# Loads, weight joins and look-ahead products moved in the first three steps of a linear-attention and feed-forward kernel

## Chip, cores and metric

The kernel runs on one core of one Trainium2 chip. The metric is the device time of one execution in microseconds (us). Matrix products run on TensorE (PE in the profile; its weight loads are PEld), elementwise work on VectorE (DVE), ScalarE (ACT) and GpSimd (POOL). SyncE (SP) only issues DMAs. Each engine works through its own queue in the order in which the program was written, because the kernel is built under a manual schedule. Semaphores are put in by the framework wherever one instruction needs what another makes, or its buffer.

## What is computed

```python
# r, k, v, w: (4, 8, 768, 48); u: (8, 48)
for t in range(S):
    cur = np.einsum('bhd,bhe->bhde', u[None] * kt, vt)
    y[:, :, t] = np.einsum('bhd,bhde->bhe', rt, state + cur)
    state = wt[:, :, :, None] * state + np.einsum('bhd,bhe->bhde', kt, vt)
x = y.transpose(0, 2, 1, 3).reshape(B * S, H * D)     # (3072, 384)
h = x @ w_in                                          # w_in (384, 2048), float64 as given
sp = np.maximum(h, 0.0) + np.log1p(np.exp(-np.abs(h)))
out = (h * erf(sp)) @ w_out                           # w_out (2048, 384), float64 as given
```

## The kernel before

The sequence is cut into six chunks of 128 tokens and the four batches into two pairs. This makes twelve steps; step `s` handles chunk `s // 2` of batch pair `s % 2`.

**Attention.** `attend_first` handles step 0, `attend` steps 1 to 4, and `attend_late` the rest. Inside a step the recurrence over time is done by halving: there are six levels. At each level PE makes 64 small products (`level_products`, L537), DVE multiplies the later halves of r and k by decay totals, in place (`scale`, L327), and DVE or ACT merges the products into the matrix `own` (`take_level`, L549 and L556). The products of level n need the scaling of level n-1, and the scaling of level n overwrites what the products of level n read. POOL makes the decay totals ahead (L349 in the first two steps, L401 in `prepare`). After level six come `from_own` (own times v into the PSUM tile `y`, L571), transposes (L896), `state_part` (L643) and `through_state` (L597), which gives xT, the transposed input of the feed-forward part. Six small DMAs fill a last part of xT (L629).

**Feed-forward.** Its work is cut into pieces that stand between the levels on PE. `hidden` of step s-1 makes the first product, 12 matmul instructions to a piece (L985). `project` of step s-3 makes the second, 8 matmul instructions to a piece (L1017). `place(n)` is called at the end of each level and issues the pieces: one hidden piece in steps 1 and 2; in step 3 two projection pieces after each of the levels one to four. From step 3 on, `project` of step 0 reads `w_out_sb`: the last two of its eight pieces, issued after level four, read its row blocks 12 to 15. The last step's projection is `project_fast`, seven products of half width with sums made by DVE (L1113, L1117).

**Weights.** They come as float64 words and are converted in 16 pairs of row blocks, 0 to 7 for `w_in_sb` and 8 to 15 for `w_out_sb`. A pair passes five stages: `l` loads the words (two DMAs, L147), `b` scales the high words on ACT into `y` (L247, L249), `r` scales the low words on ACT into a buffer `rest` (L255), `h` shifts on DVE (L264, and for pairs from 8 on a second instruction, L269), and `o` adds the rest on POOL (L277). `j` (join) is `h` and `o`. The table `CONVERT` says for each step and level which stages are sent, each time for the next pair of that stage. The first string of an entry goes out ahead of `take_level` (`early`), the second inside `place`.

**Rows for step 4.** From step 4 on, the first levels are made from rows instead. `load_rows` loads them, and `prepare(s + 1)`, a generator that is resumed once in each level of step s from level two on, multiplies them on DVE. In step 3 it is resumed between `take_level` and `place`; its resumption in level three runs from L469 on.

```python
            if level > 1 and (s, level) != (DIRECT, LOG - 1):
                next(following, None)
            place(level - 1)
```

**Buffers.** The tiles `in`, `w` and `v` have two buffers each, `words` three, `rest` two. SP issues loads in program order, so an issue that waits for a buffer holds back those behind it. `load_second`, `load_step`, `load_v` and `load_w` issue the loads of the steps.

Of the kernel before, what the change touches and what calls it, by code (L numbers as in the profile page):

```python
# [17 lines left out]
P = 128  # L18
FAST = 3
EP = 64  # L20
HC = 64
# [40 lines left out]
def kernel(  # L62
# [111 lines left out]
        nc.scalar.copy(t[:, 0, 0, 0:1], behind)  # L174
        load_halves(t, rkw[1])

    def load_v(s, behind=None):

        vt = loaded[s][1]
        if behind is not None:  # L180
            nc.gpsimd.tensor_copy(out=vt[:, 0, 0:1], in_=behind)
        nc.sync.dma_start(out=vt[:], in_=v[s])

    def load_step(s):
        t = ins.tile([P, 2, JP, C], FP32, name="in")
        vt = ins.tile([P, NH, D], FP32, name="v")
        if s < DIRECT:
            load_halves(t, rkw[s])
        else:
            nc.sync.dma_start(out=t[:], in_=rkw[s][:, 0:2])  # L190
        if s <= DIRECT:
            load_w(s)
        if s == 2:
            nc.sync.dma_start(out=block_sb[:], in_=block_mask)
            nc.sync.dma_start(out=u_row[:], in_=u_rows)
        loaded[s] = t, vt
        if s > 2:
            load_v(s)
# [16 lines left out]
    def convert(weights):  # L215

        held = {}
        plain = weights[0][1].dtype == FP32  # L220
        signed = len(weights) // 2

        def load(i, behind=None):
            if i >= len(weights):
                return
            dst, src = weights[i]
            if plain:
                nc.sync.dma_start(out=dst, in_=src)
                return
            words = wide.tile([P, 2, DM, 2], I32, name="words", bufs=3)  # L230
            if behind is not None:
                nc.gpsimd.tensor_copy(out=words[:, 0, 0, 0:1].bitcast(FP32), in_=behind)
            load_halves(words[:].rearrange("p i n two -> p i (n two)"), src.bitcast(I32))
            held[i] = {"words": words}

        def scale_high(i, part=slice(0, 2)):


            if i not in held:
                return  # L240
            if i < 2:
                base = ps_m.tile([P, NP * C], FP32, name="m")[:, :DM]
            else:
                base = y[:].rearrange("p e j q t -> p e (j q t)")[:, :, :DM]
            high = held[i]["words"][:, part, :, 1].bitcast(FP32)
            if i < signed:
                nc.scalar.activation(base, high, AF.Prelu, scale=2.0**-112, alpha=-(2.0**32))  # L247
            else:
                nc.scalar.mul(out=base, in_=high, mul=2.0**-112)  # L249
            held[i].setdefault("bases", []).append((base.bitcast(I32), part))  # L250

        def scale_low(i):
            if i in held:
                rest = wide.tile([P, 2, DM], I32, name="rest", bufs=2)
                nc.scalar.mul(  # L255
                    out=rest[:], in_=held[i]["words"][:, :, :, 0].bitcast(U32), mul=2.0**-29
                )
                held[i]["rest"] = rest

        def shift(i):  # L260
            if i in held:
                base, part = held[i]["bases"].pop(0)
                into = weights[i][0].bitcast(I32)[:, part]
                nc.vector.tensor_scalar(  # L264
                    out=into if i < signed else base, in0=base, scalar1=3, scalar2=None,
                    op0=ALU.logical_shift_left,
                )
                if i >= signed:
                    nc.vector.scalar_tensor_tensor(  # L269
                        out=into, in0=held[i]["words"][:, part, :, 1], scalar=-(1 << 31),  # L270
                        in1=base, op0=ALU.bitwise_and, op1=ALU.bitwise_or,
                    )

        def add(i):
            if i in held:
                into = weights[i][0].bitcast(I32)
                nc.gpsimd.tensor_tensor(  # L277
                    out=into, in0=into, in1=held.pop(i)["rest"][:], op=ALU.add
                )

        def join(i):
            shift(i)
            add(i)

        stages = {"l": load, "b": scale_high, "r": scale_low, "h": shift, "o": add, "j": join}
        done = {"l": 4, "b": 2, "r": 2, "j": 2}

        def send(what):
            for stage in what:
                stages[stage](done[stage])  # L290
                done[stage] += 1

        return stages, send
# [436 lines left out]
    def attend_first(xT):  # L730
# [20 lines left out]
        def wait_for(t):  # L751

            nc.gpsimd.tensor_copy(out=block_sb[:, 0:1], in_=in_t[:, 0, JP - 1, t : t + 1])
# [8 lines left out]
        for level in range(2, LOG):  # L762
            pp = turns.pop("pp", None) or products([P, NE, JP, HC])
            level_products(pp, RK, level)
            scale(0, level)
            turns["pp"] = products([P, NE, JP, HC])
            keep_busy(turns["pp"])
            take_level(own, pp, level)
            if level == 2:
                stages["b"](0, 0)  # L770
                stages["b"](0, 1)
                stages["r"](0)
                for _ in prepare(1):
                    pass
                stages["l"](1, own[:, 0, 2:3])
                nc.sync.dma_start(out=vt[:], in_=v[0])
                nc.sync.dma_start(out=ws[1][:], in_=rkw[1][:, 2])
            elif level < LOG - 1:
                stages["h"](0)
            if level in behind:  # L780
                wait_for(1 << level - 1)
                totals(*behind[level])
        totals = plan_totals(1)
        pp = turns.pop("pp")
        level_products(pp, RK, LOG)
# [27 lines left out]
        nc.scalar.copy(middle[rows(1)], ps[0][1][rows(1), :, :D])  # L813
        nc.vector.tensor_copy(middle[rows(0)], ps[0][0][rows(0), :, :D])
        stages["r"](1)
        stages["h"](1)
        stages["h"](1)
        wait_for(HC - 1)
        stages["o"](0)
        nc.gpsimd.tensor_mul(faded[1][:], middle[:], ends[:, :, 1:2].to_broadcast([P, JP, D]))  # L820
        load_v(1, middle[:, 0, 0:1])
        totals(1)
        stages["o"](1)
        totals(*range(2, LOG + 1))
# [28 lines left out]
    def attend(s, xT, early, place, behind):  # L853
# [10 lines left out]
            next(following)  # L864
        for level in range(near_log(s) + 1 if s == DIRECT else 1, LOG + 1):
            rk = made[:] if level == 1 else RK
            pp = products([P, NE, JP, HC])
            if s == level == 1:
                level_products(pp, rk, level, range(NP))
                turns.pop("hop")()  # L870
                level_products(pp, rk, level, range(NP, JP))
                send("br")
            else:
                level_products(pp, rk, level)
            if level == LOG and s == DIRECT:
                spread_blocks(s + 1, pp)
            scale(s, level)
            if s == 1 and level == 2:
                turns.pop("pending")()
                load_v(2)  # L880
            early(level - 1)
            got = pp[:].rearrange("p e n t -> p (e n) t")
            if level == 1:
                nc.vector.tensor_mul(
                    own[:], got, first[:, None, :].to_broadcast([P, NH, HC])
                )
            else:
                take_level(own, pp, level)
            if level > 1 and (s, level) != (DIRECT, LOG - 1):
                next(following, None)  # L890
            place(level - 1)

        from_own(s, own, 1)
# [184 lines left out]
    def project_fast(s, gs):  # L1078
# [34 lines left out]
        nc.vector.tensor_add(halves, halves, m0[:, None, lo].to_broadcast([P, 2, ND]))  # L1113
        nc.sync.dma_start(out=out[i * NJ + 1, c], in_=o[1][:])
        yield
        product(m1[:, lo], a12, b21, True)
        nc.vector.tensor_add(o[0][:], o[0][:], m1[:])  # L1117
        nc.sync.dma_start(out=out[i * NJ, c], in_=o[0][:])
        yield

    xTs, hids, projs = {}, {}, {}
# [58 lines left out]
    def run_late(s, tokens, following=None):  # L1180
# [26 lines left out]

    CONVERT = (
        (),
        (("j", "brl"),) * 5 + (("j", "l"), ("", ""), ("", ""), ("", "brl")),  # L1210
        (("", "jbrl"),) * 5 + (("", "j"), ("", ""), ("", ""), ("", "br")),
        (("", "jbr"), ("", "j")),
    )

    STAGES = {
# [17 lines left out]
    with tc.manual_schedule(  # L1233
# [15 lines left out]
        for s in range(n_steps):  # L1249
# [3 lines left out]
            def convert_at(n, late=True):  # L1253
                if s < len(CONVERT) and n < len(CONVERT[s]):
                    send(CONVERT[s][n][late])

            def place(n):
# [7 lines left out]
                if s in ALONE:  # L1265
                    if s == 2 and not n:

                        next(hids[0])
                    convert_at(n)
                    advance(STAGES[s][n])  # L1270
                else:
                    advance(STAGES[s][n])
                    convert_at(n)
                beside(s, next(places))

            def run(n, following):
# [12 lines left out]
                )  # L1289
            else:  # L1290
                attend_first(xTs[s])
            if s + 2 < n_steps:
                load_step(s + 2)
                if s + 2 == DIRECT:
                    load_rows(s + 2)
        s = n_steps
        from_own(s - 1, ready[s - 1][0], 1)
        fence()
# [102 lines left out]
```

## Time and profile before

| what | value |
|---|---|
| median of 3 runs (lowest, highest) | 598.27 us (597.46, 601.87) |
| the profiled execution, its own time | 599.54 us |
| its span, first to last instruction | 597.7 us |
| mean granted TensorE clock | 0.997 |
| busy share of the span: PE, PEld, DVE, ACT, POOL | 98%, 84%, 73%, 60%, 45% |
| DMA, mean over the span | 106 GB/s |

The span and what lies around it (1.8 us) make the profiled execution's time, and that stood 1.27 us above the median. Matmuls are pipelined and their ends are modelled, so PE's 98% doesn't mean that it ran at its peak; a gap between its weight loads shows a stall better. In the timeline each line gives the start and the duration in us, engine and source line, operation, output and inputs, count, and in brackets the idle time before it with what ended that. "issue" there means that the engine waited for nothing that the profile shows.

### The profile page before, as it was taken

How to read it: one execution, taken by the hardware profiler on the slowest of the kernel's cores; microseconds unless marked ns; L12 is line 12 of the kernel's file. 1: busy time of each engine (PE TensorE's matmuls, PEld its weight loads, DVE VectorE, ACT ScalarE, POOL GpSimd, SP SyncE). 2: the span in 40 equal slices, each digit the busy share in tenths (PEclk: the TensorE clock that was granted, in tenths of full speed). 3: DMA queues.
4: the chain of work that ended last, by engine and by line, in shares of the span. 5: the costliest groups of instructions: out<-in, count | busy, mean ns of one | idle time of the engine just before them, and what ended most of it. 6: DMA issues, size and time to landing. Idle time of an engine off the chain costs nothing.

```text
span 597.7 us, 16615 instructions
## 1 busy us (share of the span) xinstructions
PE 583.5 (98%) x7264; PEld 500.3 (84%) x7264; DVE 436.6 (73%) x518; ACT 361.6 (60%) x473; POOL 270.9 (45%) x306
## 2 busy tenths in 40 slices
PE   8889999999999999999999999999999999999997
PEld 6667787678758857898898898898898898898997
DVE  6757498799996799799799799799799525023140
ACT  3546777817534398675765765766666664746710
POOL 3447265510579549749549549449449100000000
PEclk9989999999999999999999999999999999999999
DMA  7685382531304324335334334334331300000000
GB/s 238 229 305 174 103 287 74 218 129 32 136 31 148 77 99 168 72 107 168 71 108 168 71 107 168 72 106 133 72 107 53 72 9 26 2 21 13 2 27 27
DMA packets 53937, 63.24 MB, mean 106 GB/s; under 512 B 35144, under 2 KB 40424, under 8 KB 52840
## 3 DMA queue, kind: packets, MB, share of 16 engines
q1 hardware_dynamic: 53480, 61.98, 32.6%
q8 instruction: 57, 0.93, 0.7%
q10 hardware_dynamic: 384, 0.20, 0.1%
q14 instruction: 16, 0.13, 0.1%
HBM read 52.39 MB, written 8.69 MB: 102 GB/s over the span
## 4 chain that ended last, share of the span: by engine, by line
PE 80%; DVE 13%; DMA 3%; issue 2%; ACT 1%; POOL 0%; SPq 0%; DVEq 0%; POOLq 0%; ACTq 0%
PE m L985 36%; PE m L1093 28%; PE m L1017 5%; PE pp L537 4%; DVE in L327 3%; PE y L571 2%; PE pp L643 2%; PE y L597 1%; DVE h L974 1%; DVE own L549 1%; DVE words L466 1%; DVE sums L452 1%; DVE y L264 1%; DVE rk L462 1%; DMA rest<-in_w_rows 1%
## 5 line engine op out<-in xcount | busy, mean ns | idle before, releaser
L985 PE MATMUL m<-xT,w_in_sb 128*128 128x256 f32 x1152 | 258.7, 383 | 1.0 <-DMA xT<-y 0.9
L985 PEld LDWEIGHTS m<-xT,w_in_sb 128*128 128x128 f32 x1152 | 216.9, 191 | 32.7 <-issue 1.3
L994 ACT COPY h<-m 128x512 f32<-128x512 f32 x96 | 55.7, 581 | 83.2 <-PE m L985 83.2
L327 DVE TENSOR_TENSOR in<-in,tot_sb 128x1024 f32<-128x1024 f32 (+1 forms) x59 | 78.3, 1327 | 26.1 <-PE pp L537 16.1
L462 POOL TENSOR_TENSOR rk<-words 128x528 f32<-128x528 f32 (+3 forms) x28 | 41.6, 1486 | 91.6 <-DVE sums L452 81.2
L466 POOL TENSOR_TENSOR words<-words,rest 128x528 f32<-128x528 f32 (+10 forms) x77 | 79.1, 1027 | 6.0
L1017 PE MATMUL m<-w_out_sb,h 128*128 128x384 f32 x192 | 64.3, 491 | 0.0
L1017 PEld LDWEIGHTS m<-w_out_sb,h 128*128 128x128 f32 x192 | 35.7, 190 | 23.6
L1093 PE MATMUL m<-mixed,h 128*128 128x192 f32 x288 | 51.1, 331 | 0.0
L1093 PE MATMUL m<-w_out_sb,h 128*128 128x192 f32 x288 | 50.3, 329 | 0.0
L941 ACT ACT_TABLE_LOAD x36 | 46.2, 1283 | 2.6 <-issue 2.0
L1093 PEld LDWEIGHTS m<-w_out_sb,h 128*128 128x128 f32 x288 | 46.9, 190 | 0.5
L1093 PEld LDWEIGHTS m<-mixed,h 128*128 128x128 f32 x288 | 46.6, 190 | 0.9
L945 ACT ACT_TABLE_LOAD x36 | 46.2, 1283 | 1.6 <-DVE room L1076 1.1
L537 PEld LDWEIGHTS pp<-in 48*64 48x64 f32 (+1 forms) x2368 | 33.6, 126 | 12.8 <-issue 6.8
L1093 PE MATMUL m<-w_out_sb,room 128*128 128x192 f32 x256 | 44.2, 326 | 0.0
L1093 PEld LDWEIGHTS m<-w_out_sb,room 128*128 128x128 f32 x256 | 42.0, 190 | 0.0
L950 DVE TENSOR_TENSOR h<-h,y 128x1024 f32<-128x1024 f32 x17 | 20.7, 1215 | 28.3 <-ACT y L945 28.2
L537 PE MATMUL pp<-in 48*64 48x64 f32 (+1 forms) x2368 | 37.9, 213 | 2.0 <-DVE in L327 2.0
L941 ACT ACTIVATE room<-h 128x1024 f32<-128x1024 f32 x36 | 38.1, 1057 | 0.4
L950 DVE TENSOR_TENSOR h<-h,pp 128x1024 f32<-128x1024 f32 x19 | 23.0, 1213 | 19.5 <-ACT pp L945 19.5
L462 POOL TENSOR_TENSOR words<-words 128x336 f32<-128x336 f32 (+6 forms) x49 | 35.2, 719 | 3.8
(141 smaller groups left out, 820.2 us busy)
## 6 DMA issues: line engine op xcount, KB each, us to landing
in<-in_rkw SPq DMA_DIRECT2D x8, 1024.0 KB, 6.0
words<-in_moe_w_in SPq DMA_DIRECT2D x16, 384.0 KB, 5.6
words<-in_moe_w_out SPq DMA_DIRECT2D x16, 384.0 KB, 4.7
words<-in_rk_rows SPq DMA_DIRECT2D x8, 768.0 KB, 5.6
w<-in_rkw SPq DMA_DIRECT2D x11, 512.0 KB, 7.4
v<-in_v SPq DMA_DIRECT2D x12, 384.0 KB, 5.8
out<-o SPq DMA_DIRECT2D x24, 192.0 KB, 2.8
in<-in_rkw SPq DMA_DIRECT2D x7, 512.0 KB, 5.9
```

The lines of the kernel that those rows point to most:

```text
L327: nc.vector.tensor_mul(halves, halves, view(tots[level - 1], 0, [[1, n], [2, nb], [0, half]]))
L462: engine.tensor_mul(terms[n], r[:, :, n:], k[:, :, : near - n])
L466: engine.tensor_mul(k[:, :, :m], k[:, :, :m], w[:, :, n : n + m])
L537: nc.tensor.matmul(pp[s0 : s0 + m, e, n, :m], lhsT=rk[rows(e), 1, n, s0 : s0 + m], rhs=rk[rows(e), 0, n, t0 : t0 + m], start=True, stop=True,)
L571: nc.tensor.matmul(y[at(e, p), e, j, p // 2, t], lhsT=vt[t, n * NE + e, :], rhs=own[t, e * JP + n, :], start=swap == 1 and not j and not q ...
L941: nc.scalar.activation(sp_room, chunks[0], AF.Softplus)
L945: nc.scalar.activation(at, sp_room, AF.Erf)
L950: nc.vector.tensor_mul(h, h, at)
L985: nc.tensor.matmul(ps[:, ff, :], lhsT=w_in_sb[:, g * FG + f + ff, kk * P : (kk + 1) * P], rhs=xT[:, kk, :], start=kk == 0, stop=kk == KT - 1,)
L994: nc.scalar.copy(h[:, f : f + FT, :], ps[:])
L1017: nc.tensor.matmul(ps[j][:], lhsT=gs[g][:, f, j * C : (j + 1) * C], rhs=w_out_sb[:, g * FG + f, :], start=g + f == 0, stop=g == NG - 1 and ...
L1093: nc.tensor.matmul(to, lhsT=a[:, f], rhs=b[:, f], start=start and f == 0, stop=f == FG - 1, skip_group_check=True,)
```

## The change

- `load_w(2)` and `load_v(1)` are issued in step 0 after level two. The POOL copy that held `load_v(1)` back goes.
- The rest of `load_step(2)` moves from the end of step 0 to step 1, level two, after the pending state product. The two small loads of `block_sb` and `u_row` move from step 2's load to step 3's. `load_rows(4)` moves from the end of step 2 to step 3, level one, after that level's join.
- The words of pair 4 are loaded in step 0, after stage `r` of pair 1, instead of in step 1.
- In `attend_first` the wait and the totals of a level come ahead of the other work of the level.
- In step 1, level six, the join of pair 7 comes ahead of `scale`.
- In step 2 the products of level two are issued right after the last piece of `hidden(0)`, ahead of that level's piece of `hidden(1)`.
- `CONVERT`: step 1 no longer loads in level one. In step 2, stages `b` and `r` of pair 13 leave level five for the end of the step, and its join leaves level six for level one of step 3. So pairs 13, 14 and 15 are joined in levels one, two and three of step 3, where pairs 14 and 15 were joined in levels one and two.
- The last sum of the last step is made and stored in two halves, the upper one ahead of the last product.

```diff
-    def load_v(s, behind=None):
+    def load_v(s):
 
         vt = loaded[s][1]
-        if behind is not None:
-            nc.gpsimd.tensor_copy(out=vt[:, 0, 0:1], in_=behind)
         nc.sync.dma_start(out=vt[:], in_=v[s])
...
-        if s <= DIRECT:
+        if 2 < s <= DIRECT:
             load_w(s)
-        if s == 2:
+        if s == 3:
             nc.sync.dma_start(out=block_sb[:], in_=block_mask)
             nc.sync.dma_start(out=u_row[:], in_=u_rows)
...
-        done = {"l": 4, "b": 2, "r": 2, "j": 2}
+        done = {"l": 5, "b": 2, "r": 2, "j": 2}
...
             take_level(own, pp, level)
+            if level in behind:
+                wait_for(1 << level - 1)
+                totals(*behind[level])
             if level == 2:
...
                 nc.sync.dma_start(out=ws[1][:], in_=rkw[1][:, 2])
+                load_w(2)
+                load_v(1)
             elif level < LOG - 1:
                 stages["h"](0)
-            if level in behind:
-                wait_for(1 << level - 1)
-                totals(*behind[level])
...
         stages["r"](1)
+        stages["l"](4)
         stages["h"](1)
...
-        load_v(1, middle[:, 0, 0:1])
         totals(1)
...
-            pp = products([P, NE, JP, HC])
+            pp = turns.pop("pp", None) or products([P, NE, JP, HC])
...
-            else:
+            elif s != 2 or level != 2:
                 level_products(pp, rk, level)
             if level == LOG and s == DIRECT:
                 spread_blocks(s + 1, pp)
+            if s == 1 and level == LOG:
+                early(level - 1)
             scale(s, level)
             if s == 1 and level == 2:
                 turns.pop("pending")()
+                load_step(2)
                 load_v(2)
-            early(level - 1)
+            if s != 1 or level < LOG:
+                early(level - 1)
...
+            if s == 2 and level == 1:
+
+                def ahead():
+                    turns["pp"] = products([P, NE, JP, HC])
+                    level_products(turns["pp"], RK, 2)
+
+                turns["ahead"] = ahead
             place(level - 1)
...
-        product(m1[:, lo], a12, b21, True)
-        nc.vector.tensor_add(o[0][:], o[0][:], m1[:])
-        nc.sync.dma_start(out=out[i * NJ, c], in_=o[0][:])
+        parts = (hi, lo) if s == n_steps - 1 else (slice(0, DM),)
+        for part in parts:
+            if part is parts[-1]:
+                product(m1[:, lo], a12, b21, True)
+            nc.vector.tensor_add(o[0][:, part], o[0][:, part], m1[:, part])
+            nc.sync.dma_start(out=out[i * NJ, c, :, part], in_=o[0][:, part])
...
-        (("j", "brl"),) * 5 + (("j", "l"), ("", ""), ("", ""), ("", "brl")),
-        (("", "jbrl"),) * 5 + (("", "j"), ("", ""), ("", ""), ("", "br")),
-        (("", "jbr"), ("", "j")),
+        (("j", "br"),) + (("j", "brl"),) * 4 + (("j", "l"), ("", ""), ("", ""), ("", "brl")),
+        (("", "jbrl"),) * 4 + (("", "jl"), ("", ""), ("", ""), ("", ""), ("", "br")),
+        (("", "jbr"), ("", "jbr"), ("", "j")),
...
                         next(hids[0])
+                        turns.pop("ahead")()
                     convert_at(n)
...
                     convert_at(n)
+                    if s == DIRECT - 1 and not n:
+                        load_rows(DIRECT)
...
-            if s + 2 < n_steps:
+            if s and s + 2 < n_steps:
                 load_step(s + 2)
-                if s + 2 == DIRECT:
-                    load_rows(s + 2)
```

## The prediction

> **What bounds the kernel now.** I read the page first, then the windows, then the timeline of steps 0 to 3 and of the end.
>
> ```profile
> PE 583.5 (98%) x7264; PEld 500.3 (84%) x7264; DVE 436.6 (73%) x518; ACT 361.6 (60%) x473; POOL 270.9 (45%) x306
> PE 80%; DVE 13%; DMA 3%; issue 2%; ACT 1%; POOL 0%; SPq 0%; DVEq 0%; POOLq 0%; ACTq 0%
> ```
>
> PE carries 80% of the chain that ended last. Work taken off another engine gains only where PE stands still; a new wait on PE costs its full length. So I list PE's stalls in the first 130 us. The windows (columns PE, PEld, DVE, ACT, POOL busy, then the granted clock) show two places:
>
> ```profile
> 36.05:39.47 3.42, 1.57 (x13) 1.38 (x14) 1.30 (x4) 0.00 (x0) 0.00 (x0) 1.00 0.68 245
> 39.47:42.89 3.42, 3.42 (x24) 2.33 (x26) 2.31 (x2) 2.05 (x3) 1.82 (x1) 0.50 0.97 329
> 109.60:126.00 16.40, 16.40 (x171) 10.08 (x172) 16.13 (x16) 9.15 (x8) 8.90 (x9) 1.00 0.35 144
> ```
>
> PE stood for half of one window and then had half its clock for the next 3.42 us. From 109.6 to 126, in step 3, DVE is busy 16.13 of 16.40 us: it has no room there. The timeline names the stalls of steps 0 to 2:
>
> ```profile
> 14.71 1.23 DVE L327 TENSOR_TENSOR in<-in,tot_sb 128x1024 f32<-128x1024 f32 x1 [0.96 <-POOL tot_sb L349]
> ...
> 30.34 0.54 PEld L537 LDWEIGHTS pp<-rk 48*64 48x64 f32 x26 [1.24 <-issue]
> ...
> 37.90 0.25 PEld L643 LDWEIGHTS pp<-v,kT 64*48 64x48 f32 x7 [2.56 <-issue]
> 38.21 4.29 PE L985 MATMUL m<-xT,w_in_sb 128*128 128x256 f32 x12
> 43.71 2.86 PE L985 MATMUL m<-xT,w_in_sb 128*128 128x256 f32 x12
> ...
> 58.40 0.55 PEld L571 LDWEIGHTS y<-own,v 64*48 64x48 f32 x32 [1.00 <-issue]
> ...
> 69.42 0.30 PEld L985 LDWEIGHTS m<-xT,w_in_sb 128*128 128x128 f32 x2 [1.28 <-issue]
> ...
> 92.64 0.66 PEld L571 LDWEIGHTS y<-own,v 64*48 64x48 f32 x32 [1.17 <-ACT own L556]
> ```
>
> And step 3, where weights meet the projection:
>
> ```profile
> 117.52 2.68 POOL L277 TENSOR_TENSOR w_out_sb<-w_out_sb,rest 128x768 int32<-128x768 int32 x1
> 119.05 1.96 DVE L469 TENSOR_TENSOR words<-words,u_row 128x768 f32<-128x768 f32 x1
> 122.42 5.43 PE L1017 MATMUL m<-w_out_sb,h 128*128 128x384 f32 x16
> 125.43 0.56 DVE L466 TENSOR_TENSOR words<-words,rest 128x384 f32<-128x384 f32 x1
> 125.91 1.22 DVE L327 TENSOR_TENSOR in<-in,tot_sb 128x1024 f32<-128x1024 f32 x1
> ```
>
> Pair 15 is finished on POOL at 120.20. Only then come the row products of step 4 on DVE, 119.05 to 125.99, and the last two projection pieces on PE at 122.42, which read it.
>
> **What the Trainium skill says.** "Runtime: NRT & Kernel Launch", Instruction fetch mechanics: instructions come in blocks of 256, the next one fetched by DMA while the current one runs, "mostly hidden". Here it is not hidden twice: from the break before 30.34 to that before 37.90 PE issues 127 weight loads, 127 matmuls and 2 waits, one block, and no operand was missing. The 57 instruction packets of queue 8 on the page fit 14,528 such instructions. "TensorE: Matmul & The Clock Gate", What's actually happening: after an idle window of about 3.4 us the clock is halved until a busy window has passed; the two windows above agree. "PSUM — Partial Sum Buffer", PSUM bank collisions: a bank is to be guarded as a whole, whatever columns are touched; no line of before shows DVE and PE at different columns of one bank. "SBUF — State Buffer", SBUF: two separate sides: DVE with two SBUF inputs and POOL exclude each other for a whole instruction; L277 takes 1.83 us alone and 2.68 at 117.52, beside L327.
>
> **The change, part by part**, against the profiled execution.
>
> *Totals ahead (step 0).* POOL's level-two totals no longer queue behind the copy that waits for `own`. The scaling at 14.71 can start when `take_level` (12.40, 1.34 us) ends, at 13.77: **-0.9**. The whole step is one chain through DVE and PE, so all behind it moves.
>
> *Loads.* `w` of step 2 (512 KB) and `v` of step 1 (384 KB) join the SP queue at 15.8. At the 350 to 400 GB/s of a busy queue they take 2.4 us and fill the lull before the next load at 23.36: nothing. The POOL copy that goes (1.18 us) freed nothing, since its totals end near 33 and PE needs them at 35. The words of pair 4 can be issued when ACT has read pair 1 (26.96, now 26.0) and `in` of step 2 right behind, when `through_state` has read its buffer. So their 1.8 MB run from about 27.5 to 32.5, where before 2.7 MB ran from 28.2 to 38. Behind them on SP, `v` of step 2 still waits for the pending product, as before. The first fetch break keeps its length: loads of pairs 2 and 3 surround it as before. The second fetch landed at 36.3 behind the loads and PE went on at 37.90. Served behind the shorter queue at 32 to 33, PE goes on at 34.5 to 35.3 and would arrive at 34.3: the break is 0.2 to 1.0 instead of 2.56 us. I take 0.8: **-1.8**; unhelped it is 0. With less than 1 us of stall the clock stays: 4.29 - 2.86 for the piece and 1.35 - 1.16 for the next level: **-1.6**, or 0.
>
> *Pair 7 ahead of scaling six.* `from_own` at 58.40 waited for the shift of pair 7 (57.38 to 58.32), because both use `y`; PE was free at 57.80: **-0.6**. The scaling, now second, waits for POOL's add until 56.38 in either order, so the transposes lose nothing.
>
> *Products ahead (step 2).* PE waited for the landing of xT from 68.5 to 70.7, in three breaks, with 0.9 us of work between. The 64 products (1.09 us) fit in, since scaling one ends at 68.11: **-1.1**.
>
> *Pair 13 out of step 2.* Its two DVE instructions (0.95 each) and two ACT ones leave the path to `from_own` at 92.64. PE was free at 91.88: **-0.8**.
>
> *Pairs 13, 14, 15 in step 3.* Pair 15 goes from level two to level three, behind the row products on DVE. That queue starts from PE's level-two products (scaling at 109.66) and is gapless to 125.99, so it moves with PE and no earlier gain helps. Shift and mask end at 125.99 + 1.90 = 127.9. POOL's add starts then, beside L327: 2.68, to 130.7 (1.83 without it: 129.8). PE comes to row block 14 after 4 of 16 instructions of 0.335 us: 122.42 + 1.34 = 123.76. Wait: **+7.0** (6.0 to 7.0). Queued behind it on PE are 12 projection instructions, level five and the pieces after it, and DVE's scaling five waits for those. An idle time of 7 us covers a whole window, so PE resumes at half clock for 3.4 to 6.8 us: +1.7 to +3.4, I take **+2.2**. DVE's own delay of 1.9 lies inside. Pairs 13 and 14 take the places of 14 and 15; nothing is late there. The rows, issued at 108.2 and 110.2, have until 119.
>
> *Last sum in halves.* DVE has to add the upper half (192 columns, about 0.33 by ACT's copy of that size) before PE may write the bank: the earlier sum ends at 592.15, then 0.33, so the last product starts at 592.57 instead of 591.18: +1.4. The last add is 0.2 shorter and its store half as large (0.1 to 0.2): **+1.0**. If columns are told apart it is -0.4.
>
> Sum: -0.9 - 1.8 - 1.6 - 0.6 - 1.1 - 0.8 + 7.0 + 2.2 + 1.0 = **+3.4**. 599.54 + 3.4 = 602.9; that execution stood 1.27 above the median, so **601.7** is the number comparable with 598.27. About 1% (6 us) is what a measurement of this kernel can tell from no change.
>
> **Rivals.** *(1) The fetch break stays.* The fetch is served by its own rule and not by queue length: at 15.99 PE entered a block with 1.6 MB queued and the packet came 1.0 us later, at 24.83 it took 3.2. Then -1.8 and -1.6 fall away: 605.1. For it: that irregularity. Against: the late fetches (27.99, 35.43, 42.79) all fall in the loaded stretch.
>
> *(2) Not slower: no wait at the last projection pieces.* If DVE joined pair 15 ahead of the row products, POOL would end near 122 and PE would not wait; -7.0 and -2.2 wouldn't be paid and the early gains, 6.8 less the end's 1.0, would stand: 592.5. The place is row block 14 in step 3; the sign turns where wait and cold clock together fall under 5.8 us. For it: only that something I haven't seen makes DVE reach it sooner. Against: the order in `attend` (resume, then `place`) and the 16.13 of 16.40.
>
> *(3) The loads do not come earlier*, because SP's queue blocks. The two issues of step 0 have free buffers; pair 4 waits for ACT at 26.0. A block would cost the same 3.4 us as (1) and is counted there.
>
> **How the numbers follow.** Forecast 0.57, its own range 599 to 604.5 (fetch 0 to 1, add 1.83 to 2.68, cold clock 1.7 to 3.4, end -0.4 to +1.0). Rival 1 with 3: 0.27, 603.5 to 607. Rival 2: 0.12, 591 to 594.5. Rest 0.04. Over 604.25: most of rival 1 and the top of the forecast, 0.25. Under 592.3: half of rival 2, 0.06. Between: 0.69. The range 594 to 606.5 leaves out most of rival 2 and the top of rival 1.
>
> **What would show it.** Right: a PE gap of 6 to 7 us at L1017 in step 3, ended by POOL L277, with a window of half clock behind it; no half clock near 40; level two of step 2 ahead of its piece; a gap of 1.4 us ahead of the last product. Wrong: no gap at L1017, then rival 2; a gap at L643 above 2 us with half clock, then rival 1. A join of pair 15 that lies ahead of L469 on DVE would end the argument.

## The result and the profile after

| | before | changed |
|---|---|---|
| median (lowest, highest), 6 runs each | 599.67 us (597.46, 601.87) | 605.13 us (604.11, 606.32) |
| ratio to before, 95% interval | 1 | 1.0095 (1.0069 to 1.0121) |
| the profiled execution, its span | 599.54, 597.7 us | 604.11, 602.3 us |

The change costs 5.5 us by the medians and 4.6 us by the two profiled executions. The prediction was made against 598.27 us, the median of the first three executions of the kernel before; three more moved that median up by 1.4 us. From the page of the changed kernel: PE's share of the chain that ended last, and the matmuls of the projection with a wait ahead of them that they didn't have before.

```profile
PE 81%; DVE 8%; ACT 6%; issue 3%; POOL 1%; ACTq 1%; DVEq 0%; POOLq 0%
...
L1028 PE MATMUL m<-w_out_sb,h 128*128 128x384 f32 x192 | 66.5, 502 | 6.5 <-POOL w_out_sb L275 6.5
```

The timelines of both kernels give the start of the same work on PE (its first weight load). Their difference shows where the time goes and comes from:

| start on PE, us | before | changed | difference |
|---|---|---|---|
| step 0, level four | 15.99 | 15.48 | -0.51 |
| step 1, level two | 33.73 | 35.11 | +1.38 |
| step 1, level three | 42.43 | 39.71 | -2.72 |
| step 1, from_own | 58.40 | 54.82 | -3.58 |
| step 2, level three | 76.56 | 71.74 | -4.82 |
| step 2, level four | 80.58 | 76.85 | -3.73 |
| step 2, from_own | 92.64 | 88.08 | -4.56 |
| step 3, level four | 121.33 | 116.63 | -4.70 |
| step 3, level five | 127.77 | 131.69 | +3.92 |
| end of the span | 597.7 | 602.3 | +4.6 |

One stretch between two levels of step 3 (15.06 us in place of 6.44) costs 8.6 us and turns 4.7 us of gain into a loss. From there to 590 us the difference stays at 3.9 us, and the end of the program adds 0.7. The PEld timeline of the changed kernel there:

```profile
116.63 1.02 PEld L535 LDWEIGHTS pp<-in 48*64 48x64 f32 x64 [0.55 <-issue]
117.72 0.94 PEld L1028 LDWEIGHTS m<-w_out_sb,h 128*128 128x128 f32 x4
125.74 0.50 PEld L1028 LDWEIGHTS m<-w_out_sb,h 128*128 128x128 f32 x2 [7.08 <-POOL w_out_sb L275]
126.55 0.34 PEld L1028 LDWEIGHTS m<-w_out_sb,h 128*128 128x128 f32 x1 [0.30 <-issue]
```

Four weight loads go out, the fifth waits 7.08 us for POOL's add (L275), and the next take 0.34 us each where they took 0.19. The DVE and POOL lines show why the add is late: the shift and mask of pair 15 (L262, L267) stand behind the row products, which run from 114.73 on.

```profile
114.73 1.97 DVE L467 TENSOR_TENSOR words<-words,u_row 128x768 f32<-128x768 f32 x1
...
120.94 0.96 DVE L262 TENSOR_SCALAR y<-y 128x768 int32<-128x768 int32 x1
121.94 0.95 DVE L267 SCALAR_TENSOR_TENSOR w_out_sb<-words,y 128x768 int32<-128x768 int32 x1
122.81 1.22 DVE L325 TENSOR_TENSOR in<-in,tot_sb 128x1024 f32<-128x1024 f32 x1
123.04 2.65 POOL L275 TENSOR_TENSOR w_out_sb<-w_out_sb,rest 128x768 int32<-128x768 int32 x1 [7.16 <-DVE w_out_sb L267]
```

The add takes 2.65 us with L325, which started 0.23 us earlier on DVE, beside it; an add of the same size with no such instruction beside it, at 22.96, takes 1.81 us. The windows (PE, PEld, DVE, ACT, POOL busy, then the clock) show the cold clock behind the wait:

```profile
122.00:125.40 3.40, 0.00 (x0) 0.00 (x0) 3.40 (x4) 0.00 (x0) 2.36 (x1) 0.61 0.00 0
125.40:128.80 3.40, 3.06 (x5) 1.84 (x6) 3.19 (x7) 0.09 (x1) 1.40 (x2) 0.50 0.02 5
```

PE does nothing in the first and has half its clock in the second (the clock was already halved from 122.74 on, while PE still waited). The end of the program, where the last sum is made in halves:

```profile
595.51 0.56 DVE L1124 TENSOR_TENSOR o<-o,m 128x384 f32<-128x384 f32 x1 [10.31 <-issue]
595.99 0.35 DVE L1131 TENSOR_TENSOR o<-o,m 128x192 f32<-128x192 f32 x1
596.38 2.57 PEld L1104 LDWEIGHTS m<-w_out_sb,h 128*128 128x128 f32 x16 [1.26 <-DVE o L1131]
```

PE waits 1.26 us for DVE to finish with the other columns of the tile `m`. It is a semaphore that holds PE back; no run shows what would happen without it.

### The profile page after: what moved, and what is told of

The parts are those of the page before. It is cut to its first block, busy times and chain, and to the rows that moved or that the text cites. A ratio compares the mean times of both kernels' runs of the same rounds, so it can differ in the third digit from the quotient of the medians.

```text
span 602.3 us, 16616 instructions
## 1 busy us (share of the span) xinstructions
PE 584.2 (97%) x7264; PEld 500.6 (83%) x7264; DVE 436.8 (73%) x519; ACT 361.5 (60%) x473; POOL 272.5 (45%) x305
## 4 chain that ended last, share of the span: by engine, by line
PE 81%; DVE 8%; ACT 6%; issue 3%; POOL 1%; ACTq 1%; DVEq 0%; POOLq 0%
PE m L996 39%; PE m L1104 27%; PE pp L535 5%; PE m L1028 3%; PE y L569 2%; PE pp L641 2%; DVE in L325 1%; PE y L595 1%; PE m L839 1%; DVE words L464 1%; DVE rk L460 1%; DVE h L985 1%; ACT room L952 1%; PE pp L907 1%; DVE own L547 1%
## 5 line engine op out<-in xcount | busy, mean ns | idle before, releaser
L325 DVE TENSOR_TENSOR in<-in,tot_sb 128x1024 f32<-128x1024 f32 (+1 forms) x59 | 79.7, 1351 | 25.1 <-PE pp L535 22.1
L1028 PE MATMUL m<-w_out_sb,h 128*128 128x384 f32 x192 | 66.5, 502 | 6.5 <-POOL w_out_sb L275 6.5
L1028 PEld LDWEIGHTS m<-w_out_sb,h 128*128 128x128 f32 x192 | 36.6, 195 | 31.4 <-POOL w_out_sb L275 7.1
```

The costliest lines, as they stand in the source:

```text
L325: nc.vector.tensor_mul(halves, halves, view(tots[level - 1], 0, [[1, n], [2, nb], [0, half]]))
L1028: nc.tensor.matmul(ps[j][:], lhsT=gs[g][:, f, j * C : (j + 1) * C], rhs=w_out_sb[:, g * FG + f, :], start=g + f == 0, stop=g == NG - 1 and ...
```

## Experiments

My theory after the result: PE waits for the late join of pair 15, then runs cold, and this outweighs the early gains. The rival: one more join on a DVE that has no room in step 3 costs the time, whatever pair it is. The first four kernels tell these apart, the next four test the early gains and the end, the last three what is worth keeping.

**e1_pairs_back.** The stages of steps 2 and 3 as before.

```diff
-        (("", "jbrl"),) * 4 + (("", "jl"), ("", ""), ("", ""), ("", ""), ("", "br")),
-        (("", "jbr"), ("", "jbr"), ("", "j")),
+        (("", "jbrl"),) * 5 + (("", "j"), ("", ""), ("", ""), ("", "br")),
+        (("", "jbr"), ("", "j")),
```

> The changed kernel with its table of conversion stages for steps 2 and 3 as it was before: pair 13 joined in step 2, level six, and pairs 14 and 15 in levels one and two of step 3; all else changed. Theory (PE waits for pair 15, then runs cold): the gap of 7.08 us at row block 14 and the half clock behind it go, 8.6 us; the start of from_own in step 2 is 0.8 later again; so 7.8 us less than the changed kernel, near 597.3. Rival (the loss comes from one more join on a full DVE in step 3, whatever pair it is): DVE loses 1.9 us of work there, so about 1.9 less, near 603.

Measured: 598.97 us, ratio to before 0.9991 (0.9973 to 1.001), 6.2 us less than the changed kernel. The PEld timeline has no gap at L1028:

```profile
119.24 1.02 PEld L535 LDWEIGHTS pp<-in 48*64 48x64 f32 x64 [0.55 <-issue]
120.33 4.81 PEld L1028 LDWEIGHTS m<-w_out_sb,h 128*128 128x128 f32 x16
125.77 1.02 PEld L535 LDWEIGHTS pp<-in 48*64 48x64 f32 x64 [0.62 <-DVE in L325]
```

From level four to level five it is 6.53 us in place of 15.06. The 8.6 us are gone but for 0.1, so the theory holds; but the time is 1.7 us above the 597.3 expected. In this execution PE's lead over the kernel before was 2.0 us at level five of step 3, where the changed kernel had gained 4.7 us by level four, and 0.2 us at the end.

**e2_join_first.** The same number of joins in step 3, pair 15's ahead of the row products.

```diff
-        (("", "jbr"), ("", "jbr"), ("", "j")),
+        (("", "jbr"), ("", "jbr"), ("j", "")),
```

> The changed kernel, but pair 15 is joined in step 3, level three, ahead of take_level and so ahead of the row products, instead of behind them. DVE has the same instructions in step 3. Theory: the gap at row block 14 falls to under 1 us and the clock stays whole; DVE's extra 1.9 us now shows as about 1.4 us of PE waiting ahead of level five and some 0.5 later; so 6 to 7 us less than the changed kernel, near 598.7. Rival (a full DVE): nothing is taken off DVE, so within 1 us of the changed kernel.

Measured: 600.05 us, ratio 1.0007 (0.9987 to 1.0026). DVE has the same instructions in step 3 as in the changed kernel, and still 5.1 us go (6 to 7 were expected). The wait at L1028 is 0.90 us, and the delay of the row products shows in the next line:

```profile
120.77 3.52 PEld L1028 LDWEIGHTS m<-w_out_sb,h 128*128 128x128 f32 x12 [0.90 <-POOL w_out_sb L275]
...
126.70 1.34 PEld L535 LDWEIGHTS pp<-in 48*64 48x64 f32 x64 [2.42 <-DVE in L325]
```

The rival is refuted as the main cause, but a full DVE has a price: 2.42 us of waiting where I expected 1.4, and a window of half clock behind it:

```profile
123.89:127.30 3.41, 1.61 (x44) 0.86 (x45) 3.34 (x6) 0.48 (x1) 0.00 (x0) 1.00 0.45 118
127.31:130.72 3.41, 3.41 (x46) 2.84 (x37) 3.20 (x8) 0.00 (x0) 0.00 (x0) 0.50 0.94 365
```

**e3_pairs_alone.** The kernel before with this part of the change alone (the table above the other way round, `load_rows(4)` moved with it).

> The kernel before with one part of the change alone: pair 13 out of step 2, pairs 13, 14, 15 joined in levels one, two, three of step 3, and the row loads of step 4 behind the join of pair 13, as they need its buffer. Theory: +8.6 for the wait and the cold clock, -0.8 for from_own in step 2: 7.8 us more than the kernel before, near 607. Rival (a full DVE): about 2 us more.

Measured: 605.94 us, ratio 1.0116 (1.0077 to 1.0155): 6.3 us more by the medians, 7.0 by the ratio, where 7.8 were expected. The gap stands in a kernel that has nothing else of the change:

```profile
127.99 0.50 PEld L1017 LDWEIGHTS m<-w_out_sb,h 128*128 128x128 f32 x2 [7.43 <-POOL w_out_sb L277]
```

So this part alone makes the kernel slower by as much as the whole change does, or a little more.

**e4_warm.** Products in the wait that nobody reads.

```diff
+                    if not s and g == NG - 1 and not j and f == FG - 2:
+                        turns["pp"] = products([P, NE, JP, HC])
+                        for _ in range(10):
+                            nc.tensor.matmul(
+                                turns["pp"][:].rearrange("p e n t -> p (e n) t")[:, :DM],
+                                lhsT=ident[:], rhs=w_in_sb[:, 0, :], start=True, stop=True,
...
```

> The changed kernel with ten extra products of 128x128 by 384 columns (two instructions of 0.335 us each, 6.7 us in all) on PE between row blocks 13 and 14 of the last but one projection piece of step 3, written to the idle product tile and read by nobody. They fill the wait and add nothing to what is waited for. Theory: the wait stays, but PE is busy in it, the clock is not halved, and the four instructions from row block 14 on and those behind run at full speed: 1.9 us less than the changed kernel. If the slow instructions behind the wait have another cause than the clock, the time stays the same or grows by what the extra products overhang.

Measured: 604.3 us, ratio 1.0086 (1.0057 to 1.0114), 0.8 us less than the changed kernel. The intervals of the two overlap, so the reading rests on the trace. The windows:

```profile
122.80:126.20 3.40, 3.40 (x13) 1.94 (x12) 3.33 (x5) 0.00 (x0) 0.74 (x1) 1.00 0.00 0
126.20:129.60 3.40, 2.87 (x10) 1.46 (x9) 3.33 (x5) 0.00 (x0) 3.02 (x2) 1.00 0.00 0
```

The clock stays whole. From level four to level five (118.54 and 132.23) it is 13.69 us against 15.06, 1.4 us less. But in this execution DVE and POOL came 0.5 us later against PE: row block 14 starts 9.62 us behind level four, against 9.11 in the changed kernel. So the clock is read from what follows the wait:

```profile
128.16 3.52 PEld L1036 LDWEIGHTS m<-w_out_sb,h 128*128 128x128 f32 x12 [1.14 <-POOL w_out_sb L275]
132.23 1.02 PEld L535 LDWEIGHTS pp<-in 48*64 48x64 f32 x64 [0.55 <-issue]
```

These twelve products take 4.07 us to level five, against 5.95 (125.74 to 131.69) in the changed kernel. So 1.9 us of the 8.6 were the cold clock, as expected, and the other 6.7 the wait.

**e5_late_w_v** and **e6_pair4_held.** Loads of the first steps, moved one group at a time.

In e5:

```diff
                 nc.sync.dma_start(out=ws[1][:], in_=rkw[1][:, 2])
-                load_w(2)
-                load_v(1)
...
                 load_step(2)
+                load_w(2)
+                load_v(1)
                 load_v(2)
```

In e6:

```diff
         stages["r"](1)
-        stages["l"](4)
         stages["h"](1)
...
+            if s == level == 1:
+                stages["l"](4, own[:, 0, 2:3])
```

> The changed kernel, but w of step 2 and v of step 1 are loaded behind in of step 2 (step 1, level two) instead of in step 0. Theory (each break of PE at the end of a block of 256 instructions is a late fetch behind queued loads, so moving loads moves breaks): the breaks at instructions 705 and 961 of PE, which the changed kernel and its variants showed with up to 2.1 and 1.5 us, fall under 0.1 us, as between 16 and 23 us no load is queued any more; those at 1217 and 1473 are 1 to 1.5 and 1 to 2.6 us. Their sum stays between 2.5 and 4, and the time within 1.5 us of the changed kernel. Rival (the early break comes from something else that was reordered in step 0): breaks at 705 or 961 remain.

> The changed kernel, but the words of pair 4 are held back by a POOL copy until own of step 1, level one, is there (about 33 us), and in of step 2, behind them on SP, with them. Theory (queued loads delay the fetch): when PE enters the block that begins at instruction 1217, about 29 to 31 us, only the loads of pairs 2 and 3 are left, so the break at 1473 is under 0.2 us in place of up to 1.35; the breaks before it stay; some 1 us less than the changed kernel or the same. Rival (the fetch takes its own time whatever is queued): a break of 1 to 2.6 us at 1473.

Measured: 605.89 us, ratio 1.0101 (1.008 to 1.0123), and 606.89 us, ratio 1.0113 (1.009 to 1.0136); neither differs from the changed kernel by more than the intervals. What they tell is where PE breaks off. The changed kernel, at the break that has grown most:

```profile
31.72 0.54 PEld L535 LDWEIGHTS pp<-rk 48*64 48x64 f32 x26 [3.02 <-issue]
```

The table gives the time from one PE instruction to the next at the ends of four blocks of 256, in us, from the records of each profiled execution. PE's instructions (weight loads, products and waits) are counted in order; e9 to e11 are described further on.

| kernel | 705 | 961 | 1217 | 1473 | sum | half clock before 45 us |
|---|---|---|---|---|---|---|
| before | 0.00 | 0.00 | 1.32 | 2.64 | 3.96 | 3.4 us from 39.5 |
| e3 (same first steps) | 0.00 | 0.00 | 1.02 | 2.64 | 3.66 | none |
| changed | 0.00 | 0.12 | 3.10 | 0.03 | 3.25 | none |
| e1 (same first steps) | 0.00 | 1.50 | 0.05 | 1.35 | 2.90 | 3.4 us from 27.2 |
| e2 (same) | 1.12 | 0.02 | 1.45 | 1.00 | 3.59 | none |
| e4 (same) | 2.05 | 0.02 | 1.72 | 0.03 | 3.82 | 3.4 us from 33.2 |
| e7 (same) | 0.00 | 0.60 | 0.91 | 1.55 | 3.06 | 3.4 us from 36.7 |
| e8 (same) | 0.76 | 0.57 | 1.18 | 3.19 | 5.70 | 3.4 us from 38.8 |
| e5 | 0.00 | 0.00 | 1.43 | 1.55 | 2.98 | 3.4 us from 36.5 |
| e6 | 0.48 | 0.29 | 0.91 | 0.03 | 1.71 | none |
| e9 (first steps of e6) | 0.00 | 0.69 | 2.27 | 0.03 | 2.99 | 3.4 us from 32.4 |
| e10 (first steps of e6) | 0.00 | 0.67 | 1.99 | 0.03 | 2.69 | none |
| e11 (loads as before) | 0.01 | 0.00 | 1.15 | 1.55 | 2.71 | none |

The loads of `w` and `v` in step 0 go with a break at 705 or 961: of the nine executions that have them eight show one of 0.4 us or more, and of the four without them (before, e3, e5, e11) none does. With pair 4 and `in` held back (e6, e9, e10) nothing breaks at 1473; but the changed kernel and e4 have no break there either. Both fit the theory, and the traces point to what PE waited for. The instruction packets of queue q8 hold 16 KB each. At all 30 breaks of 0.2 us or more in the table, PE went on 1.2 to 1.6 us after the end of such a packet; in the changed kernel the packet ended at 30.30 and PE went on at 31.72.

The same first steps break off in different places and lengths from one execution to the next. Six executions of the changed order sum to 3.7 us in the mean, two of the old order to 3.8: moving the loads moved the breaks. e6 was only 0.5 us ahead of the changed kernel at `from_own` of step 1 (54.32 against 54.82), with 1.5 us less in breaks: PE waited 1.01 us ahead of its weight loads at 47.67, where the changed kernel has no such gap.

**e7_erf_later.** `2: (1, 0, 0, ...)` in STAGES becomes `2: (0, 1, 0, ...)`.

> The changed kernel, but ScalarE's erf of 128x2048 with its table load (3.2 us) goes out in step 2 one level later. Theory (the products issued ahead bring two feed-forward pieces together on PE, and the third one waits for ACT to empty a PSUM buffer, which erf holds up): the gap of 1.16 to 1.5 us ahead of the piece in step 2, level three, goes, and the 1.2 us that the look-ahead had gained stay: 1.2 us less than the changed kernel, with the wait for pair 15 unchanged. If the gap moves to the next level, no gain.

Measured: 606.44 us, ratio 1.011 (1.0086 to 1.0135). The gap moved to the next level and grew. First the changed kernel, then this one:

```profile
74.06 2.46 PEld L996 LDWEIGHTS m<-xT,w_in_sb 128*128 128x128 f32 x12 [1.30 <-ACT h L1005]
```

```profile
79.74 2.46 PEld L996 LDWEIGHTS m<-xT,w_in_sb 128*128 128x128 f32 x12 [1.91 <-ACT h L1005]
```

The gain that was expected did not come; the other case that the expectation names did. In either place PE comes to a piece whose PSUM buffer ACT has not yet emptied, with 3.2 us of table load and erf ahead of that copy in ACT's queue.

**e8_whole_sum.** The halves of the last sum taken out.

> The changed kernel with the last sum made and stored whole again. Theory (PE may not write the bank while DVE reads other columns of it): the gap of 1.26 us ahead of the last product goes and the last sum and store are larger: 0.7 to 1.0 us less from the last DVE sum but one to the end. If columns were told apart: 0.4 us more.

Measured: 605.85 us, ratio 1.0104 (1.0078 to 1.013), within the spread. In the trace no gap precedes the last product; from the start of the last sum but one to the end of the span it is 6.2 us (599.92 to 606.1) against 6.8 (595.51 to 602.3). The halves cost 0.6 us; 0.7 to 1.0 were expected.

**e9_without_losses, e10_no_look_ahead, e11_two_edits.** e9 joins e1, e6 and e8; e10 is e9 without the products ahead in step 2; e11 is the kernel before with only these two edits:

```diff
             take_level(own, pp, level)
+            if level in behind:
+                wait_for(1 << level - 1)
+                totals(*behind[level])
             if level == 2:
...
+            if s == 1 and level == LOG:
+                early(level - 1)
             scale(s, level)
...
-            early(level - 1)
+            if s != 1 or level < LOG:
+                early(level - 1)
```

> The changed kernel without what the runs showed to cost: table of steps 2 and 3 as before, last sum whole, pair 4 and in of step 2 held back to about 33 us. Theory: what is left of the early gains stands alone: totals ahead 0.9, pair 7 ahead 0.7, shorter fetch breaks 1 to 2, look-ahead nothing since ACT takes it back: 2.5 to 3.5 less than the kernel before, near 596.5. If the early gains are lost again on the way through DVE in step 4, 0 to 1 less.

> The kernel of e9_without_losses, but the products of level two in step 2 stand behind the piece again, as in the kernel before. Theory (what the look-ahead gains on PE in step 2, level one, ACT takes back within two levels): within 0.5 us of that kernel. If the look-ahead was worth its 1.1 us: 1.1 more.

> The kernel before with two edits alone: the totals of a level ahead of its other work in step 0, and pair 7's join ahead of scaling six in step 1. Expected: 0.9 from the first (gap ahead of scaling three gone) and 0.7 from the second (gap ahead of from_own), 1.5 us less than the kernel before, near 598.1; breaks at the ends of blocks and the half clock stay as before and spread the times.

Measured against 599.87 us: e9 598.33, ratio 0.9973 (0.9957 to 0.9989); e10 598.21, 0.9975 (0.996 to 0.999); e11 597.81, 0.9975 (0.9959 to 0.999). All three are about 1.5 us faster than the kernel before by the ratio and not apart from one another. e11 did what was expected. So the two edits alone reach what any kernel here gained, and they beat both kernels. e9 fell 1 us short of its expectation; the look-ahead is worth nothing that can be measured, as e10 expected. e9 and e10 may come to their time in another way than e11: their mean granted clock was 0.999 or more in 26 of 44 executions, that of e11 in 9 of 22, that of the kernel before in 18 of 59. Holding pair 4 back seems to spare half clock; what they lose in its place stays open.

## Why the prediction came out as it did

The direction, the main mechanism and the range were right: 605.13 lies in 594 to 606.5, and the wait for POOL's add with half clock behind it stands where it was foretold. The forecast of 601.7 was 3.4 us low, and outside its own range of 599 to 604.5. Of this, 1.4 us lie in the 598.27 that it started from. As differences, the forecast said +3.4, the first rival +6.8, and measured is +5.5 (4.1 to 7.3 by the interval). That the time equals the rival's 605.1 is luck in part. A measurement told more than the 1% that was assumed: its interval is 0.5% wide. Step by step:

- **Pair 15** was expected at +7.0 for the wait; the gap between the weight loads was 7.08 and the delay that it made 6.7, by the chain foretold: row products, shift, mask, and the add beside L325. The cold clock was expected at +2.2. It lasted 6.83 us, but PE stood idle for the first 3 of them, and e4 puts its cost at 1.9. Together 8.6 against 9.2. One reading was off without effect: in the kernel before the row products start at 119.05, ahead of the end of pair 15's add at 120.20, not after it; what mattered was that pair 15's part on DVE was done by then. e2 supports "DVE's own delay lies inside": only once the long wait is gone does it show.
- **Totals ahead**, -0.9: the scaling started at 14.19 with all of the step 0.36 later by then, so 0.9 was gained. **Pair 7**, -0.6: the gap ahead of `from_own` fell from 1.00 to 0.33 us. **Pair 13 out of step 2**, -0.8: -3.73 at level four, -4.56 at `from_own`. These held.
- **Loads**, -1.8 and -1.6: this is the step that failed. I took the queue to matter at one break only and held that the first break "keeps its length"; it grew from 1.24 to 3.02 us, while the second went. "They fill the lull: nothing" was wrong too: in five of six executions of this order these two loads broke PE off at 705 or 961 by 0.6 us or more, where e5 has no break.

  Over the executions the sum of the breaks is what it was, and the clock, which I took to stay whole, was halved ahead of 45 us in four of the six. More executions say the same: the mean granted clock was 0.997 or less in 8 of the 14 of e1, and in 20 of the 38 of the kernel before that were run with it. Its price had not been set too high: those 38 took 598.1 us in the mean at 0.999 or more and 600.4 at 0.996 or 0.997, though longer breaks may go with it. With the loads and the products ahead at nothing, and the other parts as measured, the sum is -0.9 - 0.6 - 0.8 + 8.6 + 0.6 = +6.9, inside the interval. The first rival had the outcome right, that these gains are missing, but its reason fits in part only: the breaks did move with the loads.
- **Products ahead**, -1.1: right for PE at the place looked at (-3.58 to -4.82), but the next bound was not asked for. ACT took 1.1 back a level later (-3.73), and e10 lost nothing without them.
- **Last sum in halves**, +1.0: 0.6 by e8. The wait was there (1.26 us); the cost of the whole end was 0.4 smaller than I took it.

Not settled: why the same order of loads and instructions breaks off PE now at one end of a block, now at another. The traces show that PE went on shortly after an instruction packet each time, and that the place moves with the loads; they do not show what makes a packet late. Nor is it known why the profiled execution of the changed kernel lost only 4.6 us. It had no half clock ahead of step 3 and was the fastest of its six, but three of the other five had the same mean clock (0.994) and took 605.05 to 606.32 us.

## What to carry to other kernels

When an instruction is moved on an engine that works in program order, find what stands between its old and its new place in that engine's queue and count all of it against the consumer: two instructions of 0.95 us, moved behind 6.3 us of row products, cost PE 6.7 us of waiting and 1.9 us of cold clock. A gain on the bounding engine lasts only as far as its next supplier can follow, so ask which engine must now deliver sooner. And where loads are moved, do not book a gain from one profiled execution: compare several executions of the same order first.

## What the runs showed of the hardware that I had not expected

- PE's breaks at instructions 705, 961, 1217 and 1473 stood exactly 256 of its instructions apart, lasted up to 3.2 us, and moved with the queued loads. The profile puts them down to "issue"; each of 0.2 us or more ended 1.2 to 1.6 us after a 16 KB packet of the instruction queue.
- The half clock starts and ends on a grid of 3.41 us: its stretches last 3.41, 6.83 or, once in e6, 10.24 us (those that the end of the program cuts off apart). A break of 2.64 us was followed by a half-clock window in the kernel before and by none in e3, whose first steps are the same.
- The prediction took the two windows of the kernel before to agree with a whole idle window ahead of half clock. They don't: in the 3.4 us ahead of a half-clock window PE had been busy for 1.57 us (before) and 1.61 us (e2), so it need not be idle throughout.
- Ten products that nobody reads, put into a wait of 7 us, kept the clock whole.
